# Linear attention: single banks for the first item's transposes, numerators ahead of keys-values, the decode's minimum on GpSimd

## The chip, the cores and the metric

One core of a Trainium2 chip. The metric is the device time of one execution, in microseconds, from inputs in device memory to the output in device memory. The profile's times are counted from the start of the span.

## The reference

Three layers, one behind the other. Only the first one and the weights of the second are touched here.

```python
def _attn_ref(q, k, v, w_phi):            # q, k, v: 8 x 8 x 576 x 64; w_phi: 64 x 128
    def phi(x):
        proj = np.einsum('bhsd,df->bhsf', x, w_phi)
        proj = proj - np.max(np.abs(proj), axis=-1, keepdims=True)
        return np.concatenate([np.exp(proj), np.exp(-proj)], axis=-1)
    q_p, k_p = (phi(q), phi(k))
    kv = np.einsum('bhsf,bhsd->bhfd', k_p, v)
    z = np.sum(k_p, axis=2)
    num = np.einsum('bhsf,bhfd->bhsd', q_p, kv)
    den = np.einsum('bhsf,bhf->bhs', q_p, z)[..., None] + 1e-06
    return num / den

def _moe_ref(x, w_in, w_out):             # 4608 tokens, 512 -> 2048 -> 512; the weights are float64
    h = x @ w_in
    return (h * np.cos(h)) @ w_out
# then a routed layer of 8 experts, each token through its best one
```

## The kernel before

**Attention** is cut into 16 items, each two batches by two heads, and an item into five groups of token blocks (GR: two, two, one, two, two blocks of 128). It is a generator: `begin(m)` (five times) brings the first item up, then `step(j, m)` runs for items 1 to 16 and groups 0 to 4, each step in two halves with a `yield` behind each. In step (j, m) the work of three items stands side by side. The first half issues the projections of q and k for group m of item j (`proj`: TensorE into the two-bank tiles pj and pjk, then on VectorE the absolute maximum, L161, and the subtraction, L162), the transposes of the output of an earlier group (`outT`, in the other half of pjk), the transposes of q's projected values (`qexp`, into the tile "tr") and of the raw q or k of item j+1 (`turn`, also into "tr"), with ScalarE's copies and exponentials out of them. The second half issues keys-values (`kv`, L201: 16, 32 or 48 matmuls into one bank), the numerators (`num`, L240, for item j-1), on ScalarE the copy of finished sums (`kvfin`) and k's exponentials (`kexp`), and on VectorE the division (L245 to L247).

All of this is issued with `keep`, which holds each engine to the order in which the program names its instructions. Instructions without it are placed by a planner, which may move them ahead of others on their engine. Dependencies follow the tiles: a write to a tile waits for the reads of it that were issued before.

In the first item the transposes are made whole: `whole` takes the two banks of "tr" in turn. The projections of q and k of a group go into one tile, pj for even and pjk for odd groups, q in the first half of each bank and k in the second; group 1 has a form of its own (`by_bank`), and group 4 takes both tiles.

**The decode.** The second layer's weights come as float64 and are taken apart into two float32 parts, 32 pieces of 128x512. Of one piece: d[0] scales the high words (ScalarE, L459), d[1] takes a minimum (VectorE, L460), d[2] shifts (L461), d[3] and d[4] merge the low words and the sign (L462, L463, both reading the staged words and the tile), d[5] rounds (ScalarE, L464), d[6] subtracts (GpSimd while attention runs, VectorE later, L465). `decodes` runs 21 pieces beside attention, one part of four behind the second half of a step (in a few steps two); `decode` and `decode_part` run the other eleven beside the second layer's first pieces. The last steps of attention are woven with the second layer's first matmuls (L517).

In `route1`, far behind, the token numbers are copied into a record (L648). That copy depends only on constants that GpSimd makes at the start, and it isn't pinned.

Of the kernel before, what the change touches and what calls it, by code (L numbers as in the profile page):

```python
# [11 lines left out]
F32 = mybir.dt.float32  # L12
# [8 lines left out]
P = 128  # L21
# [24 lines left out]
def attention(tc, ctx, S, ident, q, k, v, w_phi, xt):  # L46
# [7 lines left out]
    pp=pctx.enter_context(tc.tile_pool(name="a_ps",bufs=1,space=PSUM))  # L54
    pk=ctx.enter_context(tc.tile_pool(name="a_kv",bufs=1,space=PSUM,side="right"))
    pj,pjk=(pp.tile([P,2,512],F32,tag=n,name=n) for n in ("pj","pjk"))
    tr=pk.tile([P,2,512],F32,tag="tr",name="tr")
    flat=itertools.count()

    w2=ap.tile([P,F],F32,name="w2",bufs=1)  # L60
    for i in range(2): tc.keep_in_program_order(nc.scalar.dma_start(w2[i*D:(i+1)*D,:],w_phi))
# [61 lines left out]
    def over(dst,c,src):  # L123

        for r in range(2): keep(nc.tensor.transpose(dst[:,r,c*H:(c+1)*H],src[r*H:(r+1)*H],ident[r*H:(r+1)*H,r*H:(r+1)*H]))
    def got(dst,a,c): return dst[:,:,a*H:c*H].rearrange("p r (c t) -> p c r t",t=H)
    def like(x): return x.rearrange("p (c r t) -> p c r t",r=2,t=H)
    def whole(srcs):

        pt=tr[:,next(flat)%2,:]  # L130
        for c,x in enumerate(srcs): keep(nc.tensor.transpose(pt[:,c*P:(c+1)*P],x,ident))
        return pt
    def turn(i,m,pt=None,base=0):
# [14 lines left out]
        return vec  # L148

    ts={}  # L150
    def proj(i,g,t,out,o=0):
        c0,n=GR[g]
        x=T[t,i]
        for c in range(n):
            for s in range(2):
                keep(nc.tensor.matmul(out[:,s,o+c*F:o+(c+1)*F],x[s*D:(s+1)*D,(c0+c)*P:(c0+c+1)*P],w2[s*D:(s+1)*D,:],start=True,stop=True))  # L156
        tt=ts[t,i,g]=S(t+"t",f"t_{t}_{i}_{g}")
        def vec():
            gg=out[:,:,o:o+n*F].rearrange("p s (c f) -> p s c f",f=F)
            m=ap.tile([P,4],F32,tag=t+"m",name=f"m_{t}_{i}_{g}")[:,:2*n].rearrange("p (s c) -> p s c",s=2)  # L160
            keep(nc.vector.tensor_reduce(m,gg,AX.X,ALU.max,apply_absolute_value=True))  # L161
            keep(nc.vector.tensor_tensor(tt[:,:n*256].rearrange("p (s c f) -> p s c f",s=2,f=F),gg,  # L162
                m.unsqueeze(3).to_broadcast([P,2,n,F]),ALU.subtract))
        return vec
    def by_bank(i,g,out):
        ms=[]
        for s in range(2):
            ms.append(ap.tile([P,4],F32,tag="qk"[s]+"m",name=f"m_{s}_{i}_{g}"))
            keep(nc.vector.tensor_reduce(ms[s],out[:,s,:].rearrange("p (c f) -> p c f",f=F),AX.X,ALU.max,apply_absolute_value=True))
        for o,t in ((0,"q"),(1,"k")):  # L170
            for s in range(2):
                keep(nc.vector.tensor_tensor(ts[t,i,g][:,s*256:(s+1)*256].rearrange("p (c f) -> p c f",f=F),out[:,s,o*256:(o+1)*256].rearrange("p (c f) -> p c f",f=F),
                    ms[s][:,2*o:2*o+2].unsqueeze(2).to_broadcast([P,2,F]),ALU.subtract))
# [30 lines left out]
    def kvfin(i,bb):  # L204

        pt=kvp.pop((i,bb))
        kz=kvs[i,bb]=S("kvh",f"kvz_{i}_{bb}")[:,:4*E1].rearrange("p (g d) -> p g d",d=E1)
        keep(nc.scalar.copy(kz,pt[:,:4*66].rearrange("p (g d) -> p g d",d=66)[:,:,:E1]))

    qx={}  # L210
    def qexp(i,g):

        n=GR[g][1]; tt=ts.pop(("q",i,g))
        srcs=[tt[:,(s*n+c)*F:(s*n+c+1)*F] for c in range(n) for s in range(2)]
        w=2*n*P
        x=ap.tile([P,1024],F32,tag="qx",name=f"qx_{i}_{g}",bufs=4)
        qx[i,g]=x[:,:2*w].rearrange("p (k h c) -> p k h c",h=2,k=2)
        if i==0 and g<3:
            pt=whole(srcs)
            made=[(x[:,kk*w:(kk+1)*w],pt[:,:w]) for kk in range(2)]  # L220
        else:
            for c,y in enumerate(srcs): over(tr,4+c,y)
            made=[(like(x[:,kk*w:(kk+1)*w]),got(tr,4,4+2*n)) for kk in range(2)]
        def vec():
            for (o,p),sign in zip(made,(1.0,-1.0)): keep(nc.scalar.activation(o,p,AF.Exp,scale=sign))
        return vec

    xss={}; xos={}
    def num(i,g):
# [20 lines left out]
    def outT(i,g):  # L250

        t0,n=GR[g]
        if g==0: xos[i]=ap.tile([P,9*P],F32,tag="xo",name=f"xo_{i}")
        xo=xos[i]; xs=xss.pop((i,g))
        po,base=(pjk,4) if (i,g)<(NI-1,0) else (tr,2*(g%2))
        for t in range(n): over(po,base+t,xs[:,t*P:(t+1)*P])
        def vec():
            keep(nc.scalar.copy(like(xo[:,t0*P:(t0+n)*P]),got(po,base,base+n)))
            if g==4:
                bp,hp=items[i]  # L260
                nc.sync.dma_start(xt[hp,:,bp*1152:(bp+1)*1152],xo)
        return vec
# [8 lines left out]
    def begin(m):  # L271

        for i,n in FIRST[m]: turn(i,n)()
        if m>1:
            kexp(0,m-2); qexp(0,m-2)()
        loads(0,m)
        yield
        if m==4: vecs=[proj(0,m,"q",pj),proj(0,m,"k",pjk)]
        else:
            out=(pj,pjk)[m%2]  # L280
            vecs=[proj(0,m,"q",out),proj(0,m,"k",out,256)]
            if m==1: vecs=[lambda: by_bank(0,m,out)]
        if m<1: warm(3)
        if m>1: kv(0,m-2)
        for f in vecs: f()
        if m==4: kvfin(0,0)
        yield
    def step(j,m):

        vecs=[]; dve=[]  # L290
        i,g=at(j,m-2); oi,og=at(j-1,m-2); ki,kg=at(j,m-1)
        if j<NI: dve.append(proj(j,m,"q",pj))
        if oi>=0: vecs.append(outT(oi,og))
        if j<NI: dve.append(proj(j,m,"k",pjk))
        two=j==1 and m==0
        if two: vecs+=[lambda: kexp(0,3),turn(2,0,pjk,4)]
        if i<NI: last=qexp(i,g)
        if two: vecs.append(turn(1,4,tr))
        elif j+1<NI: vecs.append(turn(j+1,m,tr))
        if i<NI: vecs.append(last)  # L300
        for f in vecs+dve: f()
        loads(j,m)
        yield
        if i<NI: kv(i,g)
        last=num(j-1,m)
        if i<NI and g in (2,4): kvfin(i,g//4)
# [80 lines left out]
def moes(tc, ctx, consts, S, ident, att, end_att, xt, w_in, w_out, x1d, tab, wgt, w1, w2, out):  # L387
# [61 lines left out]
    def begin():  # L449

        f,which=next(todo)
        decoded[0]+=1
        v=st[f,which].rearrange("p (f w) -> p f w",w=2)
        H=v[:,:,1]; L=v[:,:,0]
        t=xtile("gl" if decoded[0]<=20 else "row",f"d_t{which}_{f}",F32)
        ti=t.bitcast(I32)
        h,l=pair(wtag[which][f],f"w{which}_{f}")
        (win,wout)[which][f]=(h,l)
        return [lambda: pinned(nc.scalar.activation(t,H.bitcast(F32),AF.Abs,scale=2.0**-112)),  # L459
            lambda: pinned(nc.vector.tensor_scalar(t,t,F32_MAX,None,op0=ALU.min)),  # L460
            lambda: pinned(nc.vector.tensor_scalar(ti,ti,3,None,op0=ALU.logical_shift_left)),  # L461
            lambda: pinned(nc.vector.scalar_tensor_tensor(ti,L,29,ti,op0=ALU.logical_shift_right,op1=ALU.bitwise_or)),  # L462
            lambda: pinned(nc.vector.scalar_tensor_tensor(ti,H,-0x80000000,ti,op0=ALU.bitwise_and,op1=ALU.bitwise_or)),  # L463
            lambda: nc.scalar.copy(h,t),  # L464
            lambda eng: eng.tensor_tensor(l,t,f32(h),ALU.subtract)]  # L465
    def decodes(n):

        d=begin(); yield d[0]()
        for k in range(n):
            d[1](); yield d[2]()  # L470
            yield d[3]()
            d[4](); old=d
            if k+1<n:
                d=begin(); d[0]()
            yield
            pinned(old[5]()); stage(); old[6](nc.gpsimd)
            yield
    def decode():

        if decoded[0]>=2*NF: return  # L480
        d=begin()
        parts.append([lambda: (d[0](),d[1](),d[2]()), lambda: (d[3](),d[4](),d[5](),stage()), lambda: pinned(d[6](nc.vector))])
    def decode_part(n):

        for p in parts:
# [139 lines left out]
    def route1(u):  # L625
# [19 lines left out]
        nc.vector.tensor_scalar(s,s,1e-9,None,op0=ALU.add)  # L645
        rec=sb.tile([P,4,2],I32,tag="rec",name=f"rec_{u}",bufs=2)
        nc.vector.reciprocal(rec.bitcast(F32)[:,:,1],s)
        nc.vector.tensor_copy(rec[:,:,0],C["tok"].rearrange("p a c -> p (a c)")[:,4*u:4*u+4])  # L648
        ohs[u]=(oh,ob,rec)
    def route2(u):  # L650

# [470 lines left out]
```

## Time and profile before

| | us |
|---|---|
| median of 3 runs (lowest to highest) | 1583.85 (1583.15 to 1584.65) |
| the profiled execution's own time | 1583.64 |
| its span | 1581.9 |
| TensorE busy in the span | 1550.4 (98%) |
| VectorE busy | 1113.6 (70%) |
| ScalarE busy | 880.6 (56%) |
| GpSimd busy | 397.0 (25%) |

The page gives the share of each engine over the whole span; the stages differ, and the windows show them one by one. The trace gives each instruction with its start, its length and, in brackets, how long its engine stood idle ahead of it and what ended that. An instruction's length holds its latency, so neighbours on an engine can overlap a little; what one costs in a full queue is the distance from its start to the next start.

### The profile page before, as it was taken

The page shows a single profiled execution, that of the slowest core. Times are in us where ns is not written, and L with a number is a line of the kernel's source. Part 1 is how long each engine was busy: PE and PEld are TensorE (multiplying, and loading weights), DVE is VectorE, ACT ScalarE, POOL GpSimd, SP SyncE. Part 2 cuts the span into 40 slices and gives each one's busy share as a digit, 9 for nine tenths or more (in the row PEclk, how much of TensorE's full clock was granted, in tenths as well). Part 3 has the DMA queues.
Part 4 walks back from the last instruction along what each step waited for, and adds up shares of the span by engine and source line. Part 5 has one row for each costly group of instructions (what it writes and reads, how often), then busy time and mean ns, then how long its engine had stood idle before and what let it go on. Part 6 is the DMA issues. An engine that isn't in the chain of part 4 may idle for free.

```text
span 1581.9 us, 35508 instructions
## 1 busy us (share of the span) xinstructions
PE 1550.4 (98%) x14065; PEld 1339.4 (85%) x14065; DVE 1113.6 (70%) x2303; ACT 880.6 (56%) x1627; POOL 397.0 (25%) x356
## 2 busy tenths in 40 slices
PE   8899999999999999999999999999999999999998
PEld 6889898878888888888888888888899899889986
DVE  6999999968657667675767677655776656565656
ACT  6788788766434344343534344344756656565656
POOL 1111110120223433333433433334122111211212
PEclk9999999999999999999999999999999999999999
DMA  7756555233200001010101001004748667766652
GB/s 213 210 159 172 157 167 156 94 111 95 92 14 24 25 13 41 14 40 8 40 14 41 14 9 39 8 15 152 257 147 323 228 225 255 247 227 220 239 197 86
DMA packets 140850, 189.33 MB, mean 120 GB/s; under 512 B 63015, under 2 KB 87719, under 8 KB 140674
## 3 DMA queue, kind: packets, MB, share of 16 engines
q1 hardware_dynamic: 132754, 166.11, 33.6%
q0 software_dynamic: 7760, 20.79, 3.8%
q8 instruction: 113, 1.85, 0.5%
q14 instruction: 63, 0.52, 0.1%
q10 hardware_dynamic: 160, 0.07, 0.0%
HBM read 155.88 MB, written 31.82 MB: 119 GB/s over the span
## 4 chain that ended last, share of the span: by engine, by line
PE 82%; DVE 12%; DMA 4%; issue 2%; ACT 0%; SPq 0%; POOLq 0%; DVEq 0%
PE ph L517 25%; PE acc L557 19%; PE mh L825 12%; PE po L837 11%; PE acc L562 6%; DMA xg<-x1d,mrec 2%; PE kv L201 2%; DVE t_q L162 2%; DVE t_k L162 2%; DVE m_q L161 2%; DVE m_k L161 2%; PE pn L240 2%; DVE xs L247 1%; PE pjk L156 1%; PE px L807 1%
## 5 line engine op out<-in xcount | busy, mean ns | idle before, releaser
L517 PE MATMUL ph<-x,w 128*128 128x512 f32 x1728 | 418.6, 391 | 2.2 <-DVE fr L539 1.6
L517 PEld LDWEIGHTS ph<-x,w 128*128 128x128 f32 x1728 | 322.7, 188 | 70.3 <-DVE fr L539 2.0
L546 POOL TENSOR_TENSOR gl<-fr,gh 128x512 fp32r<-128x512 f32 x130 | 194.8, 1501 | 433.5 <-DVE gh L545 386.1
L780 DVE TENSOR_TENSOR m<-raw,m 128x512 fp32r<-128x512 f32 x320 | 208.2, 687 | 101.1 <-ACT m L779 73.6
L557 PE MATMUL acc<-w,gh 128*128 128x512 f32 x896 | 275.8, 389 | 0.0
L530 ACT ACTIVATE n<-ph 128x512 int32<-128x512 f32 x144 | 86.0, 597 | 272.5 <-PE ph L517 272.4
L779 ACT CAST m<-raw 128x512 fp32r<-128x512 f32 x320 | 188.1, 619 | 39.5 <-PE mh L825 32.4
L825 PE MATMUL mh<-xT,m 128*128 128x256 f32 x1728 | 201.0, 277 | 0.0
L532 DVE SCALAR_TENSOR_TENSOR fr<-ph,n 128x512 f32<-128x512 f32 x144 | 99.2, 689 | 141.9 <-ACT n L530 127.9
L825 PEld LDWEIGHTS mh<-xT,m 128*128 128x128 f32 x1728 | 197.7, 188 | 1.1 <-DVE m L780 0.8
L557 PEld LDWEIGHTS acc<-w,gh 128*128 128x128 f32 x896 | 168.2, 188 | 34.9
L837 PE MATMUL po<-m,hh 128*128 128x512 f32 x576 | 179.6, 393 | 0.0
L593 DVE SCALAR_TENSOR_TENSOR junk<-x1T,wg 128x512 f32<-128x512 f32 x224 | 179.4, 801 | 0.0
L557 PE MATMUL acc<-w,gl 128*128 128x512 f32 x448 | 174.3, 389 | 0.0
L535 ACT ACTIVATE fr<-fr 128x512 f32<-128x512 f32 x144 | 91.1, 633 | 118.1 <-DVE fr L532 118.0
L539 DVE SCALAR_TENSOR_TENSOR fr<-fr,ph 128x512 f32<-128x512 f32 x144 | 98.7, 685 | 79.7 <-ACT fr L537 79.6
L837 PEld LDWEIGHTS po<-m,hh 128*128 128x128 f32 x576 | 105.2, 188 | 19.7
L837 PE MATMUL po<-m,hl 128*128 128x512 f32 x288 | 112.4, 390 | 0.0
L886 POOL DMA_INDIRECT out_dram<-o,mrec x38 | 43.3, 1139 | 266.2 <-ACT o L885 251.9
L557 PEld LDWEIGHTS acc<-w,gl 128*128 128x128 f32 x448 | 84.1, 188 | 17.5
L201 PE MATMUL kv<-v,ke 128*64 128x65 f32 x2560 | 93.3, 225 | 0.9 <-issue 0.9
L537 ACT ACTIVATE fr<-fr 128x512 f32<-128x512 f32 x143 | 90.4, 632 | 4.3
(244 smaller groups left out, 2262.3 us busy)
## 6 DMA issues: line engine op xcount, KB each, us to landing
raw<-in_moe_w_dram SPq DMA_DIRECT2D x160, 512.0 KB, 5.8
xt<-xo SPq DMA_DIRECT2D x16, 576.0 KB, 3.7
xr<-xt SPq DMA_DIRECT2D x36, 256.0 KB, 2.9
raw_q<-in_q_dram SPq DMA_DIRECT2D x32, 256.0 KB, 4.2
raw_k<-in_k_dram SPq DMA_DIRECT2D x32, 256.0 KB, 3.8
st<-in_moe_w_in_dram SPq DMA_DIRECT2D x16, 512.0 KB, 4.2
st<-in_moe_w_out_dram SPq DMA_DIRECT2D x16, 512.0 KB, 3.7
v<-in_v_dram SPq DMA_DIRECT2D x62, 128.0 KB, 4.5
```

What stands on the lines that cost most here:

```text
L201: keep(nc.tensor.matmul(o[f0:f0+64],e[:,col+f0:col+f0+64],vh[:,h,9 if cc==4 and bb else cc,:],start=start,stop=cc==(4,8)[bb],skip_group_ch ...
L517: nc.tensor.matmul(ph,A[:,ws],xhl[u,d][k],start=n[0]==0,stop=n[0]==11); n[0]+=1
L532: ins=nc.vector.scalar_tensor_tensor(g,ph,INV2PI,n,op0=ALU.mult,op1=ALU.subtract)
L539: out0[0]=nc.vector.scalar_tensor_tensor(g,g,-0.5,ph,op0=ALU.add,op1=ALU.mult)
L546: nc.gpsimd.tensor_tensor(gl,g,f32(gh),ALU.subtract)
L557: nc.tensor.matmul(accs[u][c],A[:,ws],B,start=(f==0 and k==0),stop=(f==NF-1 and k==2))
L562: nc.tensor.matmul(accs[u][d],A[:,ws],B,start=(f==0 and k==0),stop=(f==NF-1 and k==2))
L593: return lambda: tc.keep_in_program_order(nc.vector.scalar_tensor_tensor(junk,x1T[u,c],1.0,wg[e],op0=ALU.mult,op1=ALU.mult,accum_out=lgs[u ...
L779: keep(nc.scalar.copy(h,a))
L780: keep(nc.vector.tensor_tensor(l,a,f32(h),ALU.subtract))
L825: nc.tensor.matmul(ph[:,f2*T:(f2+1)*T],A[:,ws],B[d//2][:,xs],start=n==0,stop=n==11); n+=1
L837: nc.tensor.matmul(po[c],A[:,ws],B,start=(f==0 and j==0),stop=(f==NF2-1 and j==2))
```

## The change

- The first item's transposes get a pool of two tiles of one bank each (`a_first`) in place of the two halves of "tr"; the tile "tr" of two banks is made when the first item is through.
- The first item's projections go like all others: q into pj and k into pjk. `by_bank` goes.
- `qexp` gives back its two exponentials one by one. In a step the second one is issued in the second half. There the numerators come first, then that exponential and k's, then keys-values and the copy of the finished sums, then the division.
- `outT` of the last two groups of item 14 uses "tr" in place of pjk.
- The decode's minimum is done by GpSimd, without an order, right behind d[0]; the shift stays on VectorE in the next part.
- The copy of token numbers in `route1` is pinned to its place.

```diff
@@ attention
-    tr=pk.tile([P,2,512],F32,tag="tr",name="tr")
-    flat=itertools.count()
+    first=ExitStack()
+    ps=first.enter_context(tc.tile_pool(name="a_first",bufs=2,space=PSUM,side="right"))
+    tr=[]
@@ whole
-        pt=tr[:,next(flat)%2,:]
+        pt=ps.tile([P,512],F32,tag="tr",name="flat")
@@ qexp
-        def vec():
-            for (o,p),sign in zip(made,(1.0,-1.0)): keep(nc.scalar.activation(o,p,AF.Exp,scale=sign))
-        return vec
+        def half(kk): keep(nc.scalar.activation(*made[kk],AF.Exp,scale=(1.0,-1.0)[kk]))
+        return half
@@ outT
-        po,base=(pjk,4) if (i,g)<(NI-1,0) else (tr,2*(g%2))
+        po,base=(pjk,4) if (i,g)<(NI-2,3) else (tr[0],2*(g%2))
@@ begin
-            kexp(0,m-2); qexp(0,m-2)()
+            half=qexp(0,m-2)
+            kexp(0,m-2); half(0); half(1)
...
-        if m==4: vecs=[proj(0,m,"q",pj),proj(0,m,"k",pjk)]
-        else:
-            out=(pj,pjk)[m%2]
-            vecs=[proj(0,m,"q",out),proj(0,m,"k",out,256)]
-            if m==1: vecs=[lambda: by_bank(0,m,out)]
+        vecs=[proj(0,m,"q",pj),proj(0,m,"k",pjk)]
@@ step
-        if i<NI: last=qexp(i,g)
-        if two: vecs.append(turn(1,4,tr))
-        elif j+1<NI: vecs.append(turn(j+1,m,tr))
-        if i<NI: vecs.append(last)
+        if i<NI: half=qexp(i,g)
+        if two: vecs.append(turn(1,4,tr[0]))
+        elif j+1<NI: vecs.append(turn(j+1,m,tr[0]))
+        if i<NI: vecs.append(lambda: half(0))
         for f in vecs+dve: f()
         loads(j,m)
         yield
-        if i<NI: kv(i,g)
         last=num(j-1,m)
-        if i<NI and g in (2,4): kvfin(i,g//4)
+        if i<NI: half(1)
         if ki<NI: kexp(ki,kg)
+        if i<NI:
+            kv(i,g)
+            if g in (2,4): kvfin(i,g//4)
         last()
@@ behind the first item
     for m in range(5): yield from begin(m)
+    first.close()
+    pt=ctx.enter_context(tc.tile_pool(name="a_tr",bufs=1,space=PSUM,side="right"))
+    tr.append(pt.tile([P,2,512],F32,tag="tr",name="tr"))
@@ the decode
-            lambda: pinned(nc.vector.tensor_scalar(t,t,F32_MAX,None,op0=ALU.min)),
+            lambda: nc.gpsimd.tensor_scalar(t,t,F32_MAX,None,op0=ALU.min),
...
-        d=begin(); yield d[0]()
+        d=begin(); d[0](); yield d[1]()
         for k in range(n):
-            d[1](); yield d[2]()
+            yield d[2]()
             yield d[3]()
             d[4](); old=d
             if k+1<n:
-                d=begin(); d[0]()
+                d=begin(); d[0](); d[1]()
             yield
...
-        parts.append([lambda: (d[0](),d[1](),d[2]()), lambda: (d[3](),d[4](),d[5](),stage()), lambda: pinned(d[6](nc.vector))])
+        parts.append([lambda: (d[0](),d[1]()), lambda: (d[2](),d[3](),d[4](),d[5](),stage()), lambda: pinned(d[6](nc.vector))])
@@ route1
-        nc.vector.tensor_copy(rec[:,:,0],C["tok"].rearrange("p a c -> p (a c)")[:,4*u:4*u+4])
+        pinned(nc.vector.tensor_copy(rec[:,:,0],C["tok"].rearrange("p a c -> p (a c)")[:,4*u:4*u+4]))
```

## Rows read from the trace of the kernel before

**Rows 1.** Windows: stretch, length, busy time of PE, PEld, DVE, ACT, POOL, clock, DMA.

```profile
26.00:300.00 274.00, 259.82 (x6632) 243.98 (x6632) 254.95 (x587) 221.26 (x503) 30.63 (x60) 1.00 0.60 169
...
345.00:1581.00 1236.00, 1230.69 (x6572) 1048.65 (x6570) 811.53 (x1617) 615.95 (x1035) 349.69 (x260) 1.00 0.33 109
```

**Rows 2.** Waits, 26 to 305 us: in total, times, longest.

```profile
PE pjk L125 <- DVE rd L245: 10.8, 21, 0.9
DVE rd L245 <- PE pn L240: 7.9, 17, 1.0
```

**Rows 3.** Timeline, first item: start, length, engine, line, operation, [idle before].

```profile
6.13 0.71 PE L156 MATMUL pj<-w,qT 64*128 64x128 f32 x8 [0.68 <-ACT qT L143]
...
8.34 0.17 DVE L648 COPY rec<-tok 128x4 int32<-128x4 int32 x1 [3.41 <-POOL tok L351]
8.42 0.68 DVE L161 TENSOR_REDUCE m_q<-pj 128x4 f32<-128x512 f32 x1
...
15.48 0.65 PE L131 MATMUL tr<-ident,raw_k 128*128 128x128 f32 x4 [0.68 <-ACT kT L143]
...
16.81 0.66 PE L131 MATMUL tr<-ident,t_q 128*128 128x128 f32 x4 [0.68 <-ACT kT L143]
...
18.61 0.69 DVE L161 TENSOR_REDUCE m_q<-pjk 128x4 f32<-128x512 f32 x1 [3.37 <-PE pjk L156]
...
25.72 0.68 DVE L161 TENSOR_REDUCE m_q<-pj 128x4 f32<-128x512 f32 x1
```

**Rows 4.** Timeline: the first maximum of step (15,0).

```profile
297.26 0.68 DVE L161 TENSOR_REDUCE m_q<-pj 128x4 f32<-128x512 f32 x1
```

**Rows 5.** Line L460, 26 to 305 us: length in ns (least, median, most), first, last.

```profile
L460 DVE TENSOR_SCALAR d_t<-d_t x19: 415/416/421, 34.2 to 296.5; 128x512 f32<-128x512 f32 x19
```

**Rows 6.** Timeline: a step with 48 keys-values matmuls, and the decode behind it.

```profile
163.53 1.62 PE L201 MATMUL kv<-v,ke 128*64 128x65 f32 x48
...
164.98 1.10 PE L240 MATMUL pn<-kvz,qx 128*64 128x65 f32 x32
...
166.13 0.16 DVE L245 TENSOR_SCALAR rd<-pn 128x4 f32<-128x4 f32 x1 [0.62 <-PE pn L240]
...
166.88 0.41 DVE L460 TENSOR_SCALAR d_t<-d_t 128x512 f32<-128x512 f32 x1
...
167.33 0.43 DVE L461 TENSOR_SCALAR d_t<-d_t 128x512 int32<-128x512 int32 x1
```

**Rows 7.** Timeline: GpSimd on a tile of 128x512.

```profile
9.40 0.54 POOL L1076 MEMSET zero<- 128x512 f32 x1
...
45.62 1.28 POOL L465 TENSOR_TENSOR w<-d_t,w 128x512 fp32r<-128x512 f32 x1 [12.43 <-ACT w L464]
```

**Rows 8.** Timeline: q's projections of three steps, and a wait of the first.

```profile
169.79 0.49 PE L156 MATMUL pj<-w,qT 64*128 64x128 f32 x4
...
170.52 0.23 PEld L125 LDWEIGHTS pjk<-ident,xs 64*128 64x128 f32 x4 [0.43 <-ACT ke L181]
...
173.01 0.71 PE L156 MATMUL pj<-w,qT 64*128 64x128 f32 x8
...
176.78 0.71 PE L156 MATMUL pj<-w,qT 64*128 64x128 f32 x8
```

**Rows 9.** Timeline: a decode's last merge, and VectorE beside GpSimd's subtraction.

```profile
128.06 0.67 ACT L459 ACTIVATE d_t<-st 128x512 f32<-128x512 f32 x1
...
128.81 0.68 DVE L463 SCALAR_TENSOR_TENSOR d_t<-st,d_t 128x512 int32<-128x512 int32 x1
...
429.10 0.69 DVE L593 SCALAR_TENSOR_TENSOR junk<-x1T,wg 128x512 f32<-128x512 f32 x1
...
429.36 1.59 POOL L546 TENSOR_TENSOR gl<-fr,gh 128x512 fp32r<-128x512 f32 x1 [7.37 <-DVE gh L545]
...
429.88 1.62 DVE L593 SCALAR_TENSOR_TENSOR junk<-x1T,wg 128x512 f32<-128x512 f32 x1
```

**Rows 10.** Timeline: TensorE's idle time at the end of attention.

```profile
314.60 0.34 PE L125 MATMUL pjk<-ident,xs 64*128 64x64 f32 x4 [1.60 <-DVE rd L245]
...
341.80 0.73 PE L517 MATMUL ph<-x,w 128*128 128x512 f32 x2 [1.56 <-DVE fr L539]
```

More of the change, by code (lines that the diff above doesn't have):

```diff
@@ L150, in attention, with proj @@
     ts={}
-    def proj(i,g,t,out,o=0):
+    def proj(i,g,t,out):
         c0,n=GR[g]
@@ L155, in proj @@
             for s in range(2):
-                keep(nc.tensor.matmul(out[:,s,o+c*F:o+(c+1)*F],x[s*D:(s+1)*D,(c0+c)*P:(c0+c+1)*P],w2[s*D:(s+1)*D,:],start=True,stop=True))
+                keep(nc.tensor.matmul(out[:,s,c*F:(c+1)*F],x[s*D:(s+1)*D,(c0+c)*P:(c0+c+1)*P],w2[s*D:(s+1)*D,:],start=True,stop=True))
         tt=ts[t,i,g]=S(t+"t",f"t_{t}_{i}_{g}")
         def vec():
-            gg=out[:,:,o:o+n*F].rearrange("p s (c f) -> p s c f",f=F)
+            gg=out[:,:,:n*F].rearrange("p s (c f) -> p s c f",f=F)
             m=ap.tile([P,4],F32,tag=t+"m",name=f"m_{t}_{i}_{g}")[:,:2*n].rearrange("p (s c) -> p s c",s=2)
@@ L164, in proj @@
         return vec
[L165 to L173, printed above, removed]
     es={}
@@ L221, in qexp @@
         else:
-            for c,y in enumerate(srcs): over(tr,4+c,y)
-            made=[(like(x[:,kk*w:(kk+1)*w]),got(tr,4,4+2*n)) for kk in range(2)]
-        def vec():
-            for (o,p),sign in zip(made,(1.0,-1.0)): keep(nc.scalar.activation(o,p,AF.Exp,scale=sign))
-        return vec
+            for c,y in enumerate(srcs): over(tr[0],4+c,y)
+            made=[(like(x[:,kk*w:(kk+1)*w]),got(tr[0],4,4+2*n)) for kk in range(2)]
+        def half(kk): keep(nc.scalar.activation(*made[kk],AF.Exp,scale=(1.0,-1.0)[kk]))
+        return half
     xss={}; xos={}
```

## The prediction

> **What bounds the kernel now.** I read the windows by stage first, because the share of busy time over the whole span mixes three regimes. From 345 us to the end TensorE is busy 1230.69 of 1236 us [rows 1]: that is the two feed-forward stages, nothing in the change makes a matmul there shorter, and time gained ahead of it passes through it one for one. From 26 to 300 us (attention, items 1 to 14) VectorE is busy 254.95 and TensorE 259.82 of 274 us [rows 1]: two engines nearly full, so who waits for whom decides. Then the waits of that stretch: VectorE waits for almost nothing but the numerator matmuls, 7.9 us in 17 waits, while TensorE waits 10.8 us for VectorE [rows 2]. So VectorE is the bound of a step, and it is itself stopped, now and then, by a matmul that stands late in TensorE's order. The first item (0 to 26 us) is a different thing: a chain of transposes, copies, projections and subtractions in which TensorE and ScalarE hand work back and forth and VectorE stands idle [rows 3].
>
> **First item.** Before, "tr" is one tile of two banks, and each transpose waits for the copy out of the other bank: a pair's second transposes at 15.48 (idle 0.68 for ScalarE's copy of the first), q's at 16.81 (0.68 again); VectorE then waits 3.37 us and starts its next maximum at 18.61 [rows 3]. One such turn takes 16.81 - 15.48 = 1.33 us. As two tiles of a bank each, the second transpose of a pair runs right behind the first and its copy overlaps; of the three links of a group one goes. This holds in the begins of groups 3 and 4: 2 x 1.33 = 2.7 us. In group 2 it buys nothing, since there VectorE's reductions of group 1 are last.
> The pinned routing copy (L648) is worth more than it looks: it was moved ahead to 8.34, waits 3.41 us for GpSimd's token numbers, and the first maximum starts behind it at 8.42 [rows 3]. Its data (the q projection) is there at about 6.9 (eight matmuls that start at 6.13 and take 0.71) [rows 3], so up to 1.5 us; 1.1 counted, as some of it shows again as a wait for the k projection.
> The projections in two pairs add a wait: q of group g+1 must wait for q's subtraction of group g. The first maximum would start near 7.0 and take 0.68, its subtraction end near 8.3, which is about when TensorE comes to that projection anyway (one set of transposes and the warm-up lie between): no loss. k waits until its own subtraction ends, two such instructions later, while VectorE still has the second q to do. Queued behind that wait on TensorE are the next transposes; they too wait for data of that age. Without the by-bank form six of VectorE's instructions (two maxima, four half subtractions) become four of the usual kind over the same elements: within 0.1 us.
> Sum 2.7 + 1.1 = 3.8; the second item's loads may not all have landed for transposes that come earlier, so I take 3.5, with 2.0 and 4.5 as ends.
>
> **Items 1 to 14.** From the first maximum of step (1,0) at 25.72 [rows 3] to that of step (15,0) at 297.26 [rows 4] lie 271.5 us, 19.4 an item.
> (a) The minimum. 19 of them lie there, 415 to 421 ns each [rows 5]; in the queue one costs from its start to that of the shift behind it, 167.33 - 166.88 = 0.45 us [rows 6]. Off VectorE: 19 x 0.45 = 8.6 us. What it costs on GpSimd is not in the trace. Nearest rows: a memset of the same tile takes 0.54 (no operand), the subtraction of the same pair of tiles 1.28 (two operands) [rows 7]. One operand lies between; I take 0.9. The shift then waits for GpSimd, but it is issued two steps (2 x 19.4/5 = 7.8 us) after the minimum, and GpSimd has in that time one subtraction of 1.28 and the fills of v, so VectorE and what is queued behind the shift (the next maximum) do not wait. v's fills and, behind them, SP's v loads start up to 0.9 us later, an item ahead of use: nothing.
> (b) Numerators ahead of keys-values. In the step shown the 48 keys-values matmuls take 1.62 us, the numerators run behind them at 164.98, and VectorE waits 0.62 us until 166.13 [rows 6]. With the order turned they are done 1.4 us earlier, which covers the longest such wait (1.0). All 7.9 us [rows 2] go if nothing else comes late. What is last next: keys-values stand at the step's end, their exponentials are one step old; the copy of the finished sums (kvfin) moves behind kexp on ScalarE and is needed by numerators of the next step but half a step later. The second exponential of q keeps its place on ScalarE, as nothing lies between.
> Does TensorE take over? Unhindered steps start their q projection 3.77 us apart (173.01 to 176.78); the step before it is 3.22 long with 0.43 of wait, so 2.8 [rows 8]. Of the other three kinds one is as long (3.77), one has 48 for 32 keys-values matmuls, 16 x 0.03 = 0.5 more (1.62 us for 48, rounded [rows 6]), and one has 16 of them and half of q's transposes, some 0.65 less: 3.1. An item is 4.25 + 3.77 + 2.8 + 3.77 + 3.1 = 17.7 us. VectorE comes to (271.5 - 8.6 - 7.9)/14 = 18.2. It stays the bound, by half a microsecond; the steps vary by more than that, but the heavy one comes first and is worked off in the others.
> (c) The shared port. A two-operand VectorE instruction at 429.88 took 1.62 us, not 0.69, while GpSimd's subtraction ran from 429.36 to 430.95 [rows 9]; it ended 0.55 us behind it, as if it had started only then. The decode's last merge (L463) also reads two SBUF operands, and the first instruction of the next decode, on ScalarE, ends just ahead of it: 128.06 + 0.67 = 128.73 against 128.81 [rows 9]. GpSimd's minimum would start in that gap and hold the merge back for up to its whole length. After the change VectorE no longer waits for numerators and TensorE, with ScalarE behind it, runs some 0.5 us later in a step than the release by VectorE allows (the heavy step, 4.25 against VectorE's 3.4 and a part of the decode, makes it late), except in the heavy step itself. In the other steps the merge then comes first and GpSimd waits instead. I count 0.75 us for one decode in ten: 1.5 us. In the Trainium skill, "SBUF — State Buffer", section "Who interferes with whom", the port pair that GpSimd shares with VectorE is a lock held for a whole instruction, and two SBUF inputs are enough to meet it; the row agrees. By that rule every merge that finds the minimum running loses what is left of it; taken for all of them the sum is that of the first rival.
> Sum 8.6 + 7.9 - 1.5 = 15; ends 8 (half the waits stay, the port costs 5) and 17.
>
> **End of attention.** outT of the last two groups of item 14 goes to "tr": before, it waited 1.60 us for the k pair's last subtraction [rows 10]. It now only needs "tr" free, which it is: 1.6 us. Two minima in items 15 and 16: 0.9. At 341.80 TensorE waits 1.56 us for VectorE, which has just run two decodes with two minima [rows 10]: 0.9 of that. Sum 3.4, ends 1.5 and 5. The eleven decodes after that run beside a full TensorE: nothing.
>
> **The sum.** 3.5 + 15 + 3.4 = 22 us. The profiled execution took 1583.64 us (span 1581.9), 0.2 below the median of 1583.85; 1583.64 - 22 = 1561.6, so 1562 for the median. Its own range by the ends: 1583.8 - 26 = 1557 to 1583.8 - 11.5 = 1572.
>
> **The rivals.**
> 1. The port eats the minimum. For: the gap of 0.08 us above; the pair shown [rows 9] stands for 14 of 18 decodes, in which the merge starts less than 0.7 us behind the end of that ScalarE instruction. Against: VectorE's place in the step shifts earlier. Price: 16 of 21 decodes held for about 0.85 us, 14 us, less the 1.5 already counted: 1562 + 12 = 1574. Chance 0.18.
> 2. TensorE takes over, or the waits for numerators turn into waits for the q projection behind keys-values. For: 17.7 against 18.2 is a thin margin. Then of 16.5 only the minimum's 8.6 stay: 1562 + 7 = 1569. Chance 0.10.
> 3. The other side: GpSimd's minimum is slow. Same place (the merge behind it, 16 decodes), price its full length T each. The whole gain of 23.5 without the lock is eaten from T = 23.5/16 = 1.5 us on, just above the two-operand row of 1.28; at 2.0 us the time is 1560 + 32 = 1592. Against: an operand fewer than that row. Chance 0.06.
> 4. The two single banks don't part the transposes, because something else (the landing of the loads) holds them: 1562 + 2.7 = 1565, inside the forecast's range and counted with it.
>
> **How the numbers follow.** Forecast 0.66 (1557 to 1572), rival 1 0.18, rival 2 0.10, rival 3 0.06. The range goes from 1556 to 1575: it takes in the forecast's ends, rival 2 and the middle of rival 1. A change of about 0.2% (3 us) is what a measurement can tell here. Slower by more than that: rival 3 with T above 1.7, 0.05. Within it: rivals 1 and 3 with T from 1.3 to 1.7, 0.05. Faster: 0.90.
>
> **What would show it.** The first maximum of step (1,0) near 22, not 25.7. Between the maxima of steps (1,0) and (15,0) some 256 us. VectorE's wait for the numerators under 2 us. No 1.6 us hole ahead of outT at the end. L463 at its usual 0.68 us: if many of them take over 1 us, rival 1 holds, and GpSimd's minimum has its length in the trace. If TensorE's idle time in items 1 to 14 all but goes while VectorE waits for the q projection, rival 2 does.

## The result and the profile after

The changed kernel takes 1567.63 us (median; 1565.63 to 1569.09) against 1583.5 (1581.94 to 1584.65) of the kernel before on the same chip: a ratio of 0.990, 95% interval 0.9882 to 0.9917. The profiled execution took 1569.09 us, its span is 1567.4. Predicted was 1562, with a range of 1556 to 1575: the sign and the range held, but of 22 us some 16 came (14.5 between the two profiles).

I cut the time at the marks that the prediction named: the first maximum of steps (1,0), (4,0) and (15,0), and the second layer's first accumulation. First the kernel before, then the changed one: windows with the length and the busy time of PE, PEld, DVE, ACT, POOL, the granted clock, the DMA share and GB/s.

```profile
25.72:87.28 61.56, 56.59 (x1425) 52.77 (x1426) 57.16 (x140) 47.01 (x107) 5.47 (x12) 1.00 0.72 203
87.28:297.26 209.98, 200.62 (x5135) 188.71 (x5132) 195.40 (x444) 172.25 (x394) 25.16 (x48) 1.00 0.57 161
297.26:343.79 46.53, 42.21 (x733) 35.06 (x729) 35.88 (x80) 32.12 (x66) 10.26 (x8) 1.00 0.15 49
343.79:1581.90 1238.11, 1231.90 (x6577) 1049.64 (x6575) 812.71 (x1618) 616.36 (x1036) 349.69 (x260) 1.00 0.33 109
```

```profile
22.66:83.85 61.19, 56.98 (x1426) 53.82 (x1426) 55.43 (x137) 47.08 (x107) 11.46 (x17) 0.97 0.76 210
83.85:284.53 200.68, 197.53 (x5125) 187.85 (x5121) 189.01 (x430) 171.06 (x392) 49.34 (x63) 1.00 0.59 168
284.53:329.10 44.57, 41.63 (x740) 35.09 (x737) 33.13 (x74) 31.40 (x65) 15.77 (x11) 1.00 0.16 52
329.10:1567.40 1238.30, 1232.37 (x6579) 1049.78 (x6577) 812.29 (x1612) 616.76 (x1038) 366.45 (x270) 1.00 0.33 109
```

| stretch | before | after | gain | predicted |
|---|---|---|---|---|
| first item | 25.72 | 22.66 | 3.06 | 3.5 |
| items 1 to 3 | 61.56 | 61.19 | 0.37 | 15 for items 1 to 14 |
| items 4 to 14 | 209.98 | 200.68 | 9.30 | (in the line above) |
| end of attention | 46.53 | 44.57 | 1.96 | 3.4 |
| the rest | 1238.11 | 1238.30 | -0.19 | 0 |

The rest passes everything through, as [rows 1] said. In this pair of profiles items 4 to 14 gained and items 1 to 3 gained next to nothing. In items 4 to 14 TensorE's idle time fell from 9.4 to 3.2 us.

The waits of the changed kernel, 26 to 305 us (in total, times, longest), which answer to [rows 2]:

```profile
DVE m_q L162 <- PE pj L157: 4.1, 9, 1.4
ACT d_t L451 <- DMA st<-in_moe_w_in_dram: 3.3, 1, 3.3
PE pjk L126 <- DVE rd L235: 3.2, 5, 1.7
DVE rd L235 <- PE pn L230: 1.2, 2, 0.7
```

VectorE's wait for numerators is nearly gone (7.9 to 1.2), and TensorE's wait for the division fell from 10.8 to 3.2. Two new waits matter: VectorE for the q projection, 4.1 us, and ScalarE once, 3.3 us, for a load. Lines of the first item, timeline, for [rows 3] (start, length, [idle before]), the first of them from the kernel before:

```profile
14.15 0.66 PE L131 MATMUL tr<-ident,raw_k 128*128 128x128 f32 x4
...
6.74 0.69 DVE L162 TENSOR_REDUCE m_q<-pj 128x4 f32<-128x512 f32 x1 [2.04 <-PE pj L157]
9.53 0.71 PE L157 MATMUL pjk<-w,kT 64*128 64x128 f32 x8 [0.56 <-DVE t_k L163]
13.74 1.09 PE L132 MATMUL flat<-ident,raw_k 128*128 128x128 f32 x8
15.08 0.66 PE L132 MATMUL flat<-ident,t_q 128*128 128x128 f32 x4 [0.24 <-ACT kT L144]
16.42 0.69 DVE L162 TENSOR_REDUCE m_q<-pj 128x4 f32<-128x512 f32 x1 [2.48 <-PE pj L157]
22.66 0.68 DVE L162 TENSOR_REDUCE m_q<-pj 128x4 f32<-128x512 f32 x1
```

The first maximum comes 1.68 us sooner, the pair of transposes runs in one piece, and the k projection waits 0.56 us for its own subtraction, the price that the prediction named.

### The profile page after: what moved, and what is told of

Same layout as the page of the kernel before. It is cut to its first block, busy times and chain, and to the rows that moved or that the text cites. A ratio compares the mean times of both kernels' runs of the same rounds, so it can differ in the third digit from the quotient of the medians.

```text
span 1567.4 us, 35491 instructions
## 1 busy us (share of the span) xinstructions
PE 1547.9 (99%) x14065; PEld 1340.7 (86%) x14065; DVE 1102.4 (70%) x2269; ACT 879.1 (56%) x1627; POOL 449.4 (29%) x388
## 4 chain that ended last, share of the span: by engine, by line
PE 87%; DVE 6%; DMA 4%; issue 1%; ACT 1%; POOLq 0%; SPq 0%; POOL 0%; DVEq 0%
PE ph L509 24%; PE acc L549 19%; PE mh L817 12%; PE po L829 11%; PE acc L554 6%; DMA out_dram<-o,mrec 3%; PE kv L192 3%; PE pn L230 3%; PE pj L157 2%; PE pjk L157 2%; PE tr L126 1%; DVE t_k L163 1%; DVE t_q L163 1%; DVE m_k L162 1%; DVE m_q L162 1%
## 5 line engine op out<-in xcount | busy, mean ns | idle before, releaser
L452 POOL TENSOR_SCALAR d_t<-d_t 128x512 f32<-128x512 f32 x32 | 51.9, 1621 | 192.9 <-ACT d_t L451 184.5
```

## The experiments

The decisive numbers of all profiles, in us: (1,0) is the start of that step's first maximum, the next three columns are the stretches of the table above, the last one is the median of all executions.

| kernel | (1,0) | items 1-3 | items 4-14 | end | median |
|---|---|---|---|---|---|
| before | 25.72 | 61.56 | 209.98 | 46.53 | 1583.5 |
| after | 22.66 | 61.19 | 200.68 | 44.57 | 1567.63 |
| e12_after | 22.61 | 61.70 | 199.76 | 44.53 | 1569.20 |
| e1_first | 22.55 | 61.47 | 210.01 | 46.69 | 1580.24 |
| e2_num | 26.16 | 60.52 | 204.00 | 47.21 | 1577.66 |
| e3_min | 27.88 | 60.60 | 205.92 | 45.61 | 1577.62 |
| e4_fill | 22.62 | 60.26 | 201.08 | 44.51 | 1569.20 |
| e5_parts | 22.32 | 63.45 | 198.45 | 44.58 | 1571.03 |
| e6_spread | 22.33 | 56.67 | 201.64 | 44.59 | 1566.30 |
| e7_less_dve | 21.94 | 61.18 | 197.13 | 42.90 | 1563.63 |
| e8_more_pe | 22.66 | 60.85 | 206.35 | 44.87 | 1576.98 |
| e9_out | 22.81 | 63.03 | 197.43 | 45.81 | 1571.22 |
| e10_nomin | 22.38 | 63.15 | 199.32 | 44.29 | 1568.48 |
| e11_best | 22.92 | 56.86 | 207.28 | 44.62 | 1572.51 |

Theories and rivals are named in each expectation. The kernel before, run beside e1 to e4, has a median of 1583.69, beside e5 to e8 1583.01, beside e9 to e12 1583.85. e12 is the changed kernel itself once more, and e9 is the changed kernel in all that comes ahead of step (15,0). In these three profiles of the same work items 1 to 3 took 61.19 to 63.03 us and items 4 to 14 197.43 to 200.68, but both together 260.46 to 261.87: time lost in the one can be made up in the other. So one stretch alone tells little under 3 us, their sum is steadier. e2 and e3 don't touch the first item, and their 26.16 and 27.88 are scatter too; e3's profiled execution was the slowest of its five, 1581.17 us.

**The parts one by one**, each put into the kernel before. e1, the first item alone:

```diff
-    tr=pk.tile([P,2,512],F32,tag="tr",name="tr")
+    ps=first.enter_context(tc.tile_pool(name="a_first",bufs=2,space=PSUM,side="right"))
...
+        vecs=[proj(0,m,"q",pj),proj(0,m,"k",pjk)]
...
+        pinned(nc.vector.tensor_copy(rec[:,:,0],C["tok"].rearrange("p a c -> p (a c)")[:,4*u:4*u+4]))
```

> The kernel before with only the first item's part of the change: single banks for the transposes, the projections in two pairs, the routing copy pinned. The rest (order of numerators, minimum, outT) as before. Theory A (the first item's gain is taken back by a load): the first maximum of step (1,0) comes 3 us sooner, near 22.7 instead of 25.72, but the staged weights of the third piece land near 57, as in both kernels, and ScalarE's first decode instruction, which before stood at 58.14 without a wait, can't come more than 1 us sooner; the maximum of step (4,0) then lies at 86 to 87.3 and the time at 1582 to 1583.5. Rival B (the gain passes through): the maximum of step (4,0) at 84.2, the time at 1580.5.

e2, the numerators alone:

```diff
-        if i<NI: kv(i,g)
         last=num(j-1,m)
-        if i<NI and g in (2,4): kvfin(i,g//4)
+        if i<NI: half(1)
         if ki<NI: kexp(ki,kg)
+        if i<NI:
+            kv(i,g)
+            if g in (2,4): kvfin(i,g//4)
```

> The kernel before with only the numerators ahead of keys-values (and q's second exponential behind them). Theory A (TensorE takes over): VectorE's waits for numerators (7.9 us) go, but part comes back as VectorE waiting for the q projection, so 4 to 6 us are gained: 1578 to 1580. Theory B (the waits simply go, VectorE stays the bound since it still has the minimum): 7 to 8 us, 1576.

e3, the minimum alone:

```diff
-            lambda: pinned(nc.vector.tensor_scalar(t,t,F32_MAX,None,op0=ALU.min)),
+            lambda: nc.gpsimd.tensor_scalar(t,t,F32_MAX,None,op0=ALU.min),
```

> The kernel before with only the decode's minimum on GpSimd. Theory A: VectorE is rid of 21 x 0.45 us, the minimum takes 1.5 us on GpSimd beside it and no merge is held: 6 to 9 us gained, 1575 to 1578, merges at 0.68 to 0.71 us. Theory B (the shared port): VectorE comes late in its step, as in the kernel before, so GpSimd's minimum starts in the gap ahead of the last merge and the merge takes over 1 us in most decodes: 14 x 0.8 = 11 us lost against 9 gained, 1582 to 1588. With numerators no longer hiding anything, A and B differ in the mean length of the last merge: 0.70 against 1.3 us.

The gains are 3.45, 6.03 and 6.07 us (ratios 0.9977, interval 0.9967 to 0.9987; 0.9956, 0.9943 to 0.997; 0.9963, 0.995 to 0.9977). In e1 the first item's 3.2 us pass through whole, though ScalarE waits 2.1 us for the load: theory A falls, such a wait alone costs that kernel nothing. In e2 VectorE waits 0.2 us for numerators and 2.4 for q's projection (26 to 300 us), which is theory A's mechanism; the gain stands at the upper end of its 4 to 6. Between the maxima of (1,0) and (15,0) e2 gains 7.0 and e3 5.0 us, together the change has 9.7 (10.1 in e12): some 2 us of the one are in the other. In e3 VectorE still waits 8.5 us for numerators, so it can use only part of its new room. The port costs little even there: 13 of 19 last merges took their usual time, and six took 0.86 to 1.09 us, 2.2 us more in all. The last merge in e3, 26 to 305 us (ns least/median/most), and one that was held:

```profile
L463 DVE SCALAR_TENSOR_TENSOR d_t<-st,d_t x19: 678/682/1086, 43.6 to 301.9; 128x512 int32<-128x512 int32 x19
...
87.40 1.49 POOL L460 TENSOR_SCALAR d_t<-d_t 128x512 f32<-128x512 f32 x1 [8.65 <-ACT d_t L459]
87.48 1.08 DVE L463 SCALAR_TENSOR_TENSOR d_t<-st,d_t 128x512 int32<-128x512 int32 x1
```

**Who bounds a step now**, both in the changed kernel. e7, VectorE relieved:

```diff
             yield d[2]()
-            yield d[3]()
+            yield
             d[4](); old=d
```

> The changed kernel without the decode's first merge (the three low bits of the weights decoded beside attention are left out): 21 instructions of 0.68 us fewer on VectorE, 15 of them between the maxima of steps (4,0) and (15,0). Theory A (TensorE has become the bound of a step there): that stretch shrinks from 200.7 us by 0 to 3 us, since TensorE is busy 197.5 of it. Rival B (VectorE still bounds it): it shrinks by 8 to 10 us. In items 1 to 3, four such instructions, both expect 1.5 to 2.7 us.

e8, TensorE loaded:

```diff
+        if i>0 and t=="k":
+            for s in range(2): keep(nc.tensor.matmul(out[:,s,0:F],x[s*D:(s+1)*D,c0*P:(c0+1)*P],w2[s*D:(s+1)*D,:],start=True,stop=True))
```

> The changed kernel with two of the k projection's matmuls done twice in each step of items 1 to 15 (0.09 us each, so 0.18 a step and 0.9 an item on TensorE). Theory A (TensorE bounds a step from item 4 on): the stretch between the maxima of steps (4,0) and (15,0) grows by 8 to 10 us of the 9.8 added, 200.7 to 209 to 211. Rival B (VectorE bounds it): TensorE's 3 us of idle time and VectorE's pace cover it, and it grows by at most 4.

Windows of items 4 to 14, e7 and then e8:

```profile
83.12:280.25 197.13, 195.98 (x5125) 187.26 (x5121) 182.02 (x416) 171.21 (x392) 48.06 (x63) 1.00 0.60 171
```

```profile
83.51:289.86 206.35, 206.30 (x5346) 198.68 (x5344) 190.70 (x429) 172.48 (x393) 48.28 (x63) 1.00 0.57 165
```

e7 takes 14 merges of 0.68 us, 9.6 us, off VectorE in this stretch (15 had been counted), and it is 3.6 us shorter than in the changed kernel's profile. e8 adds 8.8 us to TensorE's busy time (9.8 had been counted), and it is 5.7 us longer. Neither is the clean case. But e9, whose work in this stretch is the changed kernel's, shows how short the stretch can be without either change:

```profile
85.84:283.27 197.43, 196.91 (x5125) 187.50 (x5121) 188.51 (x429) 171.44 (x392) 49.54 (x63) 1.00 0.60 170
```

TensorE is idle for 0.5 us there. Against this profile e7 gains 0.3 us and e8 loses 8.9. In e8 itself TensorE is busy 206.30 of 206.35 us. So TensorE is the bound of these steps: theory A holds in both, and what VectorE can still hold up is at most the 3.2 us in 200 for which TensorE stands idle in the changed kernel's first profile.

**Items 1 to 3.** What the changed kernel's trace shows there, ScalarE, then TensorE:

```profile
52.72 1.17 ACT L172 ACTIVATE ke<-t_k 128x512 f32<-128x512 f32 x2
57.18 0.70 ACT L451 ACTIVATE d_t<-st 128x512 f32<-128x512 f32 x1 [3.29 <-DMA st<-in_moe_w_in_dram]
...
58.29 0.36 ACT L248 COPY xo<-pjk 128x256 f32<-128x256 f32 x1
...
57.84 0.71 PE L157 MATMUL pj<-w,qT 64*128 64x128 f32 x8
60.25 0.28 PE L126 MATMUL pjk<-ident,xs 64*128 64x64 f32 x2 [1.69 <-DVE rd L235]
61.55 2.00 PE L230 MATMUL pn<-kvz,qx 128*64 128x65 f32 x32
```

The weights of the third piece were asked for at 51.01 on SyncE's queue (SP), behind the loads of the next items and three fills of 768 KB; in the kernel before it was 50.75. ScalarE comes to them at 53.89, some 4 us sooner than before (58.14, without a wait), waits 3.29 us, and everything behind that instruction (the copy out of the k projection's tile, the exponentials) waits with it. TensorE runs dry for 1.69 us, and then its clock falls:

```profile
60.00:61.00 1.00, 0.75 (x16) 0.78 (x18) 0.93 (x5) 0.72 (x3) 0.76 (x1) 0.99 1.06 342
61.00:62.00 1.00, 1.00 (x21) 0.88 (x19) 0.96 (x3) 0.61 (x2) 0.00 (x0) 0.50 1.28 273
62.00:63.00 1.00, 1.00 (x24) 1.00 (x22) 1.00 (x2) 1.00 (x4) 0.00 (x0) 0.50 0.77 123
63.00:64.00 1.00, 1.00 (x26) 1.00 (x24) 0.93 (x4) 0.83 (x2) 0.00 (x0) 0.50 0.76 171
64.00:65.00 1.00, 1.00 (x20) 0.88 (x20) 0.97 (x3) 0.38 (x1) 0.00 (x0) 0.81 0.43 88
```

The 32 numerator matmuls at 61.55 took 2.00 us at a clock of 0.50 (the lower level, 1.2 GHz), 1.16 at full clock. That looked like the whole answer, and e4 and e5 were made to take the wait away. e4 (STAGED holds the staged loads in their order):

```diff
             for c in range(3):
+                if c: yield
                 rows = x1d[LAST + 3 * c * P : LAST + 3 * (c + 1) * P, :]
-                nc.sync.dma_start(rows.rearrange("(c p) d -> p c d", p=P), zero.unsqueeze(1).to_broadcast([P, 3, 512]))
+                behind(tc,nc.sync.dma_start(rows.rearrange("(c p) d -> p c d", p=P), zero.unsqueeze(1).to_broadcast([P, 3, 512])),STAGED[-1])
...
-        if n==25:
+        if n in (45,65): next(setup)
+        if n==85:
             for _ in setup: pass
```

> The changed kernel with three fills of 768 KB each (rows of the later table, needed only far behind) issued behind the staged loads of later pieces, three items later, instead of at 36 to 50 us. Theory A: the fills held up the staged load that ScalarE waits for at 57.18 (3.3 us), and with it went the clock at 61 to 64.4; without them ScalarE's wait is under 1 us, the clock stays at 1.00, the maximum of step (4,0) comes at 79.5 to 80.5 instead of 83.85, and the time is 1563 to 1564.5. Rival B (the attention's own loads or TensorE bound these items anyway): the wait shrinks but another takes its place, the maximum of step (4,0) at 83 or later, 1567.

e5:

```diff
-    PARTS.update({25:2,55:2,85:2,115:2,169:4})
+    PARTS.update({25:0,27:2,29:2,55:2,85:2,115:2,169:4})
```

> The changed kernel with two parts of the decode put one step later: the third piece's first instruction on ScalarE (57.18 us, 3.29 us of waiting for its staged load) comes about 4 us later in the program, and no DMA is moved. Theory A (that wait and the half clock behind it cost about 2 us net): ScalarE's wait is under 0.5 us, the granted clock stays at 1.00, the maximum of step (4,0) comes at 81.5 to 82.2 instead of 83.85, the time at 1565 to 1566. Rival B (the time is taken back within the item by VectorE, which has the setup's small instructions to do): the wait goes, but the maximum of step (4,0) stays above 83, the time at 1567.

In e4 ScalarE's wait is gone and the clock stays at 1.00, but only 0.9 us are gained at (4,0), 0.5 at (15,0), nothing in the median: rival B. Its timeline, TensorE:

```profile
74.43 0.86 PE L231 MATMUL pn<-kvz,qx 128*64 128x65 f32 x21
76.69 0.51 PE L231 MATMUL pn<-kvz,qx 128*64 128x65 f32 x10 [1.41 <-issue]
```

In the middle of the numerators TensorE stands idle for 1.41 us and waits for nothing that the trace names. The same gap, with 10 matmuls left, is in e7 (0.97), e9 (1.90), e10 (1.69), e11 (1.07) and in the changed kernel's own second profile:

```profile
78.13 0.51 PE L230 MATMUL pn<-kvz,qx 128*64 128x65 f32 x10 [1.52 <-issue]
```

In the first profile, where TensorE came there later, it is missing. So one delay had covered another; what TensorE stands for there is taken up in the last section. e5 (PARTS says how many parts of the decode go behind a half step) settles nothing: the third piece waits no more, but the fourth, asked for later, does (3.37 us at 70.52), TensorE has a gap of 1.80 us at 61.54, the clock falls again, and the time is 3.4 us more (1.8 more than e12's).

e6, the fills tied as in e4, and the setup later:

```diff
-        if n in (17,19,21,23): C=next(setup)
-        if n==25:
+        if n in (32,42,52,62): C=next(setup)
+        if n in (72,82): next(setup)
+        if n==92:
             for _ in setup: pass
```

> The changed kernel with the setup of constants (19 small VectorE instructions, 4.4 us of busy time between 22.7 and 65 us) spread over items 3 to 6 instead of items 1 and 2, and the three fills behind it. Theory A (in items 1 and 2 VectorE is the bound because of that setup; from item 4 on TensorE is, and VectorE has room): items 1 to 3 shrink from 61.2 us to 56 to 57.5, items 4 to 14 grow by at most 1.5 from 200.7, the time is 1563 to 1565. Rival B (VectorE bounds the later items too): what items 1 to 3 gain, items 3 to 6 lose, and the time stays within 1 us of 1567.5.

Windows of e6, items 1 to 3 and 4 to 14:

```profile
22.33:79.00 56.67, 55.29 (x1426) 52.60 (x1426) 52.29 (x122) 46.90 (x107) 12.01 (x16) 1.00 0.68 182
79.00:280.64 201.64, 197.59 (x5124) 187.96 (x5121) 191.17 (x445) 171.46 (x392) 49.87 (x63) 1.00 0.63 181
```

By the windows theory A: items 1 to 3 lose 4.5 us, the later ones take on the small instructions for 1.0. Of the 4.5 some 0.9 belong to the wait, by e4. The other 3.6 stand against e4, which has the gap of 1.41 us that e6 has not, so not all of them need be VectorE's setup; most are, since e11 below, with the same setup and a gap of 1.07, needs 56.86 us. In the profile the second layer's last accumulation comes 3.4 us sooner than in the changed kernel's; the medians differ by 1.3 (ratio to the kernel before 0.9898, interval 0.9883 to 0.9913), which these intervals can't tell from nothing.

**GpSimd, the end, and a last try.** e9, in the changed kernel:

```diff
-        po,base=(pjk,4) if (i,g)<(NI-2,3) else (tr[0],2*(g%2))
+        po,base=(pjk,4) if (i,g)<(NI-1,0) else (tr[0],2*(g%2))
```

> The changed kernel with the output transposes of item 14's last two groups back in the k projection's tile. Theory A (that part is worth what it removes): TensorE's hole of about 1.6 us ahead of these transposes is back, the way from the maximum of step (15,0) to the second layer's first matmul grows from 22.51 to 23.7 to 24.1 us, the time by 1.2 to 1.6. Rival B (the hole was only exchanged for the new wait of 1.20 us of the numerators for the division): it grows by less than 0.5.

The way from (15,0) to the first matmul of the second layer grows from 22.5 (307.04 - 284.53) to 24.15 us, to the first accumulation by 1.3: theory A. The median grows by 2.0 against e12, but the intervals of their ratios to the kernel before (0.9898 to 0.994 and 0.989 to 0.9922) overlap. A hole is back ahead of the transposes, and a longer one ahead of that matmul, whose bank the copy of their result holds:

```profile
300.01 0.34 PE L126 MATMUL pjk<-ident,xs 64*128 64x64 f32 x4 [0.99 <-DVE rd L235]
...
307.42 1.88 PE L509 MATMUL ph<-x,w 128*128 128x512 f32 x7 [1.58 <-ACT xo L248]
```

e10, in the changed kernel, beside e12, which is the changed kernel itself:

```diff
-            lambda: nc.gpsimd.tensor_scalar(t,t,F32_MAX,None,op0=ALU.min),
+            lambda: None,
```

> The changed kernel with the decode's minimum left out (a clamp that no weight here reaches): 32 GpSimd instructions, 51.9 us of its busy time, fewer. Theory A (GpSimd's minimum is hidden; it waits for VectorE, not the other way round): the time stays within 1 us of the changed kernel's; only the few VectorE instructions that took 1.06 to 1.10 us beside it go back to 0.43 and 0.68. Rival B (the minimum's 1.5 us on GpSimd hold the decode or the port somewhere): 3 us or more are gained.

> The changed kernel itself again, beside the three others on the same chip, so that differences of 1 us can be read: 1566 to 1569.

Without any minimum the time is 0.7 us under e12's, inside the scatter. Its 51.9 us on GpSimd are hidden, theory A.

e11, in e6:

```diff
-    PARTS.update({25:2,55:2,85:2,115:2,169:4})
+    PARTS.update({25:2,55:2,85:2,115:2,141:2,145:2,149:2,153:2})
```

> The setup of constants spread over items 3 to 6 as in the run before, and the decode's last piece (four parts in a row behind attention's last step) brought forward into items 13 to 15. Theory A (in the last steps VectorE, with those four parts in a row, keeps TensorE waiting 1.08 us ahead of the second layer): the way from the maximum of step (15,0) to the second layer's first accumulation shrinks from 44.6 to 42.5 to 43.7 us, and with the 3 us of items 1 to 3 the time is 1562.5 to 1565. Rival B (TensorE, the bound of items 13 to 15, is held up by the parts that come sooner, or another wait takes the place): 44.3 or more, and 1566.

The opposite of a gain, 207.28 us for items 4 to 14. VectorE and TensorE stand still behind ScalarE, timeline:

```profile
279.23 0.62 ACT L458 CAST w<-d_t 128x512 fp32r<-128x512 f32 x1 [3.17 <-issue]
280.15 0.69 DVE L163 TENSOR_REDUCE m_k<-pjk 128x4 f32<-128x512 f32 x1 [2.94 <-ACT xo L249]
281.72 0.28 PE L127 MATMUL pjk<-ident,xs 64*128 64x64 f32 x2 [2.58 <-DVE rd L236]
```

The rounding of a piece that was brought forward waits 3.17 us on ScalarE's ordered queue, a second time 4.87. The trace names no releaser; its target is one of the pieces laid into buffers of attention's inputs, so that it waits for attention to leave them is likely, but argued. The last stretch gains nothing either (44.62), but the second wait lies in it, at 301.59, so theory A is not tested there: from the second layer's first matmul to its first accumulation e11 needs 18.1 us (313.60 to 331.68) where the changed kernel needs 22.1, and the wait ahead of them eats that.

## Why the prediction was right, and where it was too high

**First item: 3.06 for 3.5.** The two links are there as counted. From group 3's first transposes to q's it was 16.81 - 14.15 = 2.66 us and is 15.08 - 13.74 = 1.34, and in group 4 it is 1.34 less too: 2.66 of 2.7. The routing copy, counted at 1.1, gave 0.4: the first maximum comes 1.68 us sooner, but TensorE's transposes of group 3 only 0.41 (14.15 to 13.74), as TensorE had been waiting for ScalarE there and not for that maximum. e1 shows that the sum passes through.

**GpSimd's minimum: outside its bounds, without harm.** Taken at 0.9 us, between 0.54 and 1.28 [rows 7]. It takes 1.49, more than the subtraction with its two operands; the changed kernel, 26 to 305 us:

```profile
L452 POOL TENSOR_SCALAR d_t<-d_t x20: 1487/1491/2034, 27.6 to 291.9; 128x512 f32<-128x512 f32 x20
L455 DVE SCALAR_TENSOR_TENSOR d_t<-st,d_t x19: 681/682/1105, 37.8 to 291.9; 128x512 int32<-128x512 int32 x19
```

That is the point at which rival 3 eats the gain. It did not, for one thing because of the step on the port that held: VectorE mostly comes first, and GpSimd waits. One pair of each kind:

```profile
37.77 1.51 POOL L452 TENSOR_SCALAR d_t<-d_t 128x512 f32<-128x512 f32 x1 [6.70 <-ACT d_t L451]
37.84 1.10 DVE L455 SCALAR_TENSOR_TENSOR d_t<-st,d_t 128x512 int32<-128x512 int32 x1
...
123.09 0.68 DVE L455 SCALAR_TENSOR_TENSOR d_t<-st,d_t 128x512 int32<-128x512 int32 x1
123.22 1.89 POOL L452 TENSOR_SCALAR d_t<-d_t 128x512 f32<-128x512 f32 x1 [7.83 <-ACT d_t L451]
```

1.5 us were counted for the port, 0.4 were paid there, so rival 1 is out. Even the one held merge ended at 38.94, before the minimum (39.28): it was held for 0.42 us, not for what was left of it. The Trainium skill, "SBUF — State Buffer", section "Who interferes with whom", has the later of the two blocked until the first one's instruction is through; for this one-operand minimum the row says less, and the row decides. That was not foreseen, and here it was luck: in e3, with VectorE at its old place, nine of 19 merges began while the minimum ran and lost 0.4 us at most, 2.2 in all. So rivals 1 and 3, at 0.85 and 1.49 us for each of 16 decodes, were priced too high for either order.

**Items 1 to 14: the mis-sized term, 9.7 for 15** (10.1 in e12, 11.1 in e9's profile). Two steps failed. The first is that I took 271.5 us over 14 items as 19.4 each. Before, items 1 to 3 took 20.5 and items 4 to 14 took 19.1. For the latter the sum (15 minima of 0.45 and 6.3 us of waits, 13.1 off 210) brings VectorE to 17.9 an item, below TensorE, which was busy 17.96 and came to 18.24 with its gaps; I had it at 17.7 from four kinds of steps, against 18.2 for VectorE, and called it a thin margin. It had turned over: rival 2 came, in part. 13.1 less the port became 9.3, and e7, e8 and e9 show TensorE as the bound; VectorE's waits for numerators came back in part as waits for the q projection. Rival 2's price (all of the waits lost) was too high, because TensorE could still use most of the room.

The second is items 1 to 3, where 4 minima and 1.6 us of waits, 3.4 us, gave 0.4. The prediction followed VectorE there and never asked what an earlier ScalarE would run into: a load whose time is set by the order of SP's queue. That price can't be read off alone: without the wait, 0.9 us came back (e4), while a gap of 1.4 in TensorE's stream took its place. What bounds these items most is neither, it is the setup on VectorE (e6, up to 3.6 us). How the rest divides between the load, the clock and the gap stays open, and so does how much of the shortfall belongs to these items at all: e9 lost 1.5 us in them and gained 12.5 in the others.

**End of attention: 1.96 for 3.4.** The transposes into "tr" gave 1.2 to 1.3 of 1.6 (e9). The minima gave about 0.9 (46.53 to 45.61 in e3) where 1.8 were counted. Against them stand a wait that comes with the earlier numerators, which now run into the division of the group before in their one bank (e2's end is 0.7 longer), and two VectorE instructions held beside GpSimd. Timeline, for [rows 10]:

```profile
302.01 1.15 PE L230 MATMUL pn<-kvz,qx 128*64 128x65 f32 x32 [1.20 <-DVE xs L237]
...
323.54 1.06 DVE L453 TENSOR_SCALAR d_t<-d_t 128x512 int32<-128x512 int32 x1
325.13 1.07 DVE L454 SCALAR_TENSOR_TENSOR d_t<-st,d_t 128x512 int32<-128x512 int32 x1
...
327.58 0.50 PE L509 MATMUL ph<-x,w 128*128 128x512 f32 x1 [1.08 <-DVE fr L531]
```

The hole of 1.56 us at the end became 1.08, and the one of 1.20 at 302.01 is new.

## What to carry to other kernels

Where two engines are nearly full, work out both of them for the stretch itself, not as a mean over unlike items: what comes off one is worth only the distance to the other. When a stage starts sooner, look on every ordered queue for the first instruction that waits for a transfer, for all behind it waits too (here at 57.18, in e5 at 70.52). And before a stall is given the blame, take it away: it may have been covering the next one. Add neighbouring stretches up before a single one is believed, since time lost in one can be made up in the next.

## What the runs showed of the hardware

A float32 minimum of 128x512 with one operand took 1.49 us on GpSimd and 0.42 on VectorE, while the two-operand subtraction took 1.28 on GpSimd. A two-operand merge on VectorE that started behind such a minimum lost only what was left of the minimum's first 0.48 us: in e3 0.40 us where it started 0.07 to 0.08 us behind, 0.18 at 0.30, nothing at 0.49 and 0.64. In the changed kernel the minimum took 1.89 to 1.90 us where it began 0.13 us behind the merge, and 2.03 where both began together.

After 1.69 us without work TensorE's granted clock fell to 0.50 from 61 to 64 us, although it was busy all through those three; in the second profile of the same kernel a hole of 1.37 us at the same place left it at 1.00. The length of the hole does not decide alone: behind 1.86 us in e5 and 1.90 in e9 the clock fell too, but 2.15 us in e7 and 2.57 in e10, again at the same place, left it at 1.00. e10, a matmul and a window:

```profile
60.90 0.28 PE L126 MATMUL pjk<-ident,xs 64*128 64x64 f32 x2 [2.57 <-DVE rd L235]
...
61.00:62.00 1.00, 1.00 (x24) 0.93 (x24) 0.97 (x4) 0.65 (x3) 0.00 (x0) 1.00 1.19 322
```

TensorE stopped for 0.97 to 1.90 us at one and the same instruction of the program in six profiles, and the waits name no releaser. The transfers show one thing: the DMA queue of kind "instruction" moved one packet of 16 KB just ahead of it, in the second profile of the changed kernel from 75.69 to 76.70 us (packets, MB, share of the 16 engines' time, 75.60 to 76.72 us):

```profile
q8 instruction: 1, 0.02, 5.6%
```

In all six TensorE went on 1.3 to 1.5 us behind the end of such a packet (here at 78.13), and in the first profile, without a stop, the same instruction also came 1.4 us behind one. e8, with 600 more TensorE instructions in its trace (28975 for 28375), has 115 of these packets, and all other profiles have 113. So TensorE was most likely waiting for the next block of its own code; why that block came when it did, no run here tests.
